# One-row load of `lower_bound`, turned on TensorE, and tile addresses moved to multiples of 512 bytes

## The chip, the cores and the metric

The kernel runs on one core of one Trainium2 chip. The metric is the device time of one execution in microseconds (us). Three runs of the kernel before took 201.95, 200.79 and 200.88 us; their median, 200.88 us, is the number to compare with.

## The reference

The computation has two parts. A gated recurrence runs along the sequence, for each of 4 batches and 256 channels, and its output goes through a soft mixture of experts with 32 slots (8 experts of 4). Cut to what matters:

```python
# x, f_logit: (4, 5056, 256); lower_bound: (256,); phi: (256, 32); w1: (8, 256, 1024); w2: (8, 1024, 256)
f = lower_bound + (1 - lower_bound) * sigmoid(f_logit)
i = 1 - f
for t in range(S):
    h = f[:, t] * h + i[:, t] * x[:, t]
    y[:, t] = h
logits = y.reshape(20224, 256) @ phi
d = softmax(logits, over the 20224 tokens);  c = softmax(logits, over the 32 slots)
slot_input = d.T @ y
slot_out = relu(slot_input @ w1) @ w2            # per expert
out = c @ slot_out                               # (20224, 256)
```

All inputs and the output are float32. `x` and `f_logit` are 20.7 MB each, the two weight arrays 8.4 MB each, the output 20.7 MB; `lower_bound` is 1 KB.

The kernel uses the identity 1 - f = (1 - lower_bound) * sigmoid(-f_logit). So `lower_bound` itself is needed only in two small constants per channel, `omlb` = 1 - lower_bound and `nomlb` = lower_bound - 1.

## The kernel before

**Tiling.** A unit of work is 512 tokens of one batch, 40 units in all, numbered n. The 256 channels are split as channel = 2p + o, so a partition p holds two neighbouring channels (`DC` = 2). Tokens arrive with tokens on the partitions, in 4 KB or 8 KB pieces per partition (`load`, L195 to L216). Per unit, ScalarE takes the sigmoid (`gate`, L226, tile `s_t`), GpSimd multiplies by x (`enter`, L237, tile `u_t`; the first unit is done by VectorE at L233), TensorE turns both to channels (L252, L258), ScalarE makes the decay `a` = 1 + nomlb * s (`decay`, L286 and L293), VectorE runs the scan (`scan`, L304), TensorE turns the result back to tokens (L317), a copy brings it to SBUF (L334), and TensorE makes the logits (L348) and adds up the slots (L398). Then come the experts (L590 to L686), and last the output: TensorE products (L704, L754), scaled by VectorE and ScalarE (L694, L759, L765), and stored by DMA.

**Order.** The order of all instructions on every engine is the order of the program text (`tc.manual_schedule()`). SP's queue issues the loads of `x` and `f_logit` and nearly all stores; ACT's queue issues the load of `lower_bound` (L75) and one store; GpSimd's queue issues `moe_phi` (L79) and the weights, which are converted from float32 to bfloat16 by the DMA on the way (L130, L140). The weights are issued among the late units, by the table `W_AT`. The tiles for `x` and `f_logit` are three deep, each holding two units.

**The start.** In program order: the load of `lb`, the load of `phi_f`, twelve loads for units 0 to 5 (`load(n, 1)`, 512 KB each, `f_logit` and `x` in turn), `lb_constants()`, then `gate(0)`, `enter(0)`, `s_to_channels(0)`, `decay(0)` for o = 0, and so on. `omlb` is used by `phi_constants` on GpSimd (L109) and by L598 and L599 late in the program. `nomlb` is the scale of every decay, first at L293 for unit 0. The PSUM pool `ptp` has a single buffer under the tag `tp`, used by `hp` in `to_tokens` (L317).

**Places in SBUF.** Pools are laid one after the other from the bottom of each partition's row: `consts`, `store`, `wts` (the weights), `ld` (the loaded `f_t` and `x_t`), and others above. Each tile's row is rounded up to 32 bytes. In the program before, `ident_f` begins at byte 16,512, `lb` at 17,792, `omlb` at 17,824, `nomlb` at 17,856, `phi_f` at 17,888, `etall` at 18,368, the first weight tile at 30,976 and the first `f_t` at 88,320. Once the weights are done, the output tiles `ob` and `oc` take the space from 30,976 on. From the first weight tile on, everything that a DMA reads or writes begins at 256 bytes past a multiple of 512.

Of the kernel before, what the change touches and what calls it, by code (L numbers as in the profile page):

```python
# [9 lines left out]
F32 = mybir.dt.float32  # L10
BF16 = mybir.dt.bfloat16
# [7 lines left out]
def kernel(  # L19
# [10 lines left out]
    nc = tc.nc  # L30
    B, S, D = x.shape
# [4 lines left out]
    P = 128  # L36
    DC = D // P
    FC = F // P
    R = 4
# [27 lines left out]
    consts = ctx.enter_context(tc.tile_pool(name="consts", bufs=1))  # L67
    ident_f = consts.tile([P, P], F32, name="ident_f")
# [2 lines left out]

    rep = consts.tile([P, B, NS], F32, name="rep")

    lb = consts.tile([P, DC], F32, name="lb")
    nc.scalar.dma_start(out=lb, in_=lower_bound.rearrange("(p o) -> p o", o=DC))  # L75
    omlb = consts.tile([P, DC], F32, name="omlb")
    nomlb = consts.tile([P, DC], F32, name="nomlb")
    phi_f = consts.tile([P, DC, NS], F32, name="phi_f")
    nc.gpsimd.dma_start(out=phi_f, in_=moe_phi.rearrange("(p o) s -> p o s", o=DC))  # L79
    phi = consts.tile([P, DC, NS], BF16, name="phi")  # L80
# [20 lines left out]
        nc.vector.memset(parity[ds(b * NS, NS), ds(b % 2, 1)], 1.0)  # L101

    def lb_constants():
        nc.vector.tensor_scalar(omlb, lb, -1.0, 1.0, ALU.mult, ALU.add)
        nc.vector.tensor_scalar(nomlb, lb, 1.0, -1.0, ALU.mult, ALU.add)

# [3 lines left out]


    store = ctx.enter_context(tc.tile_pool(name="store", bufs=1))
    etall = store.tile([P, S], BF16, name="etall")
    rrow = store.tile([P, n_grp * R, B], F32, name="rrow")
    left = store.tile([P, L, 2], BF16, name="left")
    nc.vector.memset(left, 0.0)
# [39 lines left out]
    with tc.tile_pool(name="sp2", bufs=3) as sp2, \  # L156
# [297 lines left out]
        for n in range(SINGLE):  # L454
            load(n, 1)
        lb_constants()
        gate(0, 1)
        enter(0)
# [368 lines left out]
```

## Time and profile before

| | |
|---|---|
| median of three runs | 200.88 us (200.79 to 201.95) |
| span of the profiled execution, first to last instruction | 198.1 us |
| lies outside the span, against the median | 2.8 us |
| busy: TensorE, VectorE, ScalarE, GpSimd | 153.3, 143.3, 138.7, 103.0 us |
| DMA packets | 14,448, 70.77 MB |
| HBM read, written | 58.23 MB, 20.71 MB |
| load of `lb`: issued, landed after | 0.72 us, 4.3 us |
| first `f_t` used (sigmoid of unit 0) | 4.85 us |
| first matmul | 6.05 us |

The profile is of one execution on the one core. Its span is what instructions cover; the time of that very execution beside the span isn't given, so that the 2.8 us between the span and the median of the other runs is taken to be what lies around a span. A "DMA share" in a row of windows is the busy share of the core's 16 DMA engines; as neighbouring packets overlap a little, a saturated stretch reads 1.02 to 1.07. The weights count in GB/s with what they write, half of what they read.

### The profile page before, as it was taken

The numbers are of one execution on the slowest core, as the hardware profiler recorded it, in microseconds if no ns is written. First come the engines' busy times: TensorE is split into PE (matmuls) and PEld (weight loads), VectorE is DVE, ScalarE is ACT, GpSimd is POOL, SyncE is SP. The second block draws the span as 40 slices with busy tenths as digits, with TensorE's granted clock in tenths as the row PEclk, the third lists the DMA queues.
The fourth block names the chain that finished last, engine by engine and source line by source line (L and its number), as shares of the span: only waits on it lengthen the run. The fifth ranks groups of instructions, "written<-read, shape, count | busy, mean of one in ns | idle before, by whom it ended". The sixth has DMA issues, their size and how long they took to land.

```text
span 198.1 us, 3497 instructions
## 1 busy us (share of the span) xinstructions
PE 153.3 (77%) x1330; PEld 110.4 (56%) x1330; DVE 143.3 (72%) x164; ACT 138.7 (70%) x195; POOL 103.0 (52%) x78
## 2 busy tenths in 40 slices
PE   0587599987999989898997978999989999950000
PEld 0366478776776768676695856568953543310000
DVE  1669869999699999999989999523268878840000
ACT  2688677899889999999897595622069889980000
POOL 2489578774998688884969969290030000000000
PEclk9999759997999999999999999999995555555555
DMA  5999999999999999999999999999639999999995
GB/s 177 418 420 419 427 429 429 427 427 357 378 424 424 408 337 420 432 411 307 407 420 392 241 215 214 213 212 211 110 110 419 430 421 427 450 443 424 424 424 218
DMA packets 14448, 70.77 MB, mean 357 GB/s; under 512 B 1744, under 2 KB 3024, under 8 KB 10464
## 3 DMA queue, kind: packets, MB, share of 16 engines
q1 hardware_dynamic: 11520, 62.00, 75.5%
q0 software_dynamic: 2624, 8.42, 21.3%
q8 instruction: 10, 0.16, 0.3%
q10 hardware_dynamic: 288, 0.13, 0.2%
q14 instruction: 6, 0.05, 0.1%
HBM read 58.23 MB, written 20.71 MB: 399 GB/s over the span
## 4 chain that ended last, share of the span: by engine, by line
PE 32%; DMA 30%; DVE 18%; POOL 6%; issue 3%; ACT 1%; ACTq 0%; SPq 0%; POOLq 0%
DMA x_t<-in_x_dram 15%; DVE h L304 13%; PE op L754 12%; DMA w_t<-in_moe_w_dram 8%; DMA w_sb<-in_moe_w_dram 7%; POOL u_t L237 5%; PE hp L317 4%; PE up L258 4%; PE sp L252 3%; DVE ht L334 3%; PE op L704 2%; PE slot_ps L174 2%; PE lg L348 1%; PE slot_ps L398 1%; DVE ob L694 1%
## 5 line engine op out<-in xcount | busy, mean ns | idle before, releaser
L237 POOL TENSOR_TENSOR u_t<-s_t,x_t 128x1024 bf16<-128x1024 bf16 (+1 forms) x39 | 82.5, 2128 | 23.3 <-ACT s_t L226 13.9
L304 DVE TENSOR_TENSOR_SCAN h<-a,h,up 128x512 bf16<-128x512 f32 (+1 forms) x72 | 86.9, 1252 | 4.7 <-PE up L258 2.5
L226 ACT ACTIVATE s_t<-f_t 128x2048 bf16<-128x2048 f32 (+2 forms) x23 | 38.3, 1668 | 5.8 <-DMA f_t<-in_f_logit_dram 4.5
L317 PE MATMUL hp<-ident_f,h 128*128 128x128 f32 (+1 forms) x160 | 29.5, 309 | 7.3 <-DVE ht L334 6.0
L317 PEld LDWEIGHTS hp<-ident_f,h 128*128 128x128 f32 (+1 forms) x160 | 23.1, 208 | 15.3 <-DVE ht L334 9.6
L252 PE MATMUL sp<-ident_f,s_t 128*128 128x128 f32 x144 | 22.6, 303 | 10.1 <-ACT s_t L226 7.8
L286 ACT ACTIVATE a<-sp,nomlb 128x1024 f32<-128x1024 bf16 x24 | 25.4, 1114 | 0.8 <-PE sp L252 0.6
L252 PEld LDWEIGHTS sp<-ident_f,s_t 128*128 128x128 f32 x144 | 18.6, 158 | 11.8 <-issue 6.0
L754 PE MATMUL op<-slot_bd,etall 64*128 64x512 bf16 x62 | 24.4, 600 | 0.1
L765 ACT ACTIVATE oc<-op,rrow 128x256 f32<-128x256 f32 x60 | 22.8, 490 | 1.4 <-PE op L754 0.9
L759 DVE TENSOR_TENSOR oc<-op,rrow 128x1024 f32<-128x1024 f32 x16 | 19.3, 1223 | 4.6 <-PE op L754 4.5
L293 ACT ACTIVATE a<-sp,nomlb 128x512 f32<-128x512 bf16 (+2 forms) x22 | 17.9, 859 | 4.8 <-PE sp L252 4.4
L258 PE MATMUL up<-ident_f,u_t 64*128 64x64 f32 x192 | 17.6, 229 | 2.0 <-POOL u_t L237 1.9
L174 PE MATMUL slot_ps<-rep,ident 128*128 128x256 bf16 x122 | 17.7, 281 | 0.0
L258 PEld LDWEIGHTS up<-ident_f,u_t 64*128 64x128 f32 x192 | 13.9, 138 | 5.9 <-POOL u_t L237 2.4
L754 PEld LDWEIGHTS <-etall 64*128 64x128 bf16 x62 | 9.0, 153 | 14.2 <-issue 11.6
L334 ACT COPY ht<-hp 128x512 f32<-128x512 f32 (+1 forms) x18 | 10.4, 580 | 8.0 <-PE hp L317 7.9
L334 DVE COPY ht<-hp 128x512 f32<-128x512 f32 (+1 forms) x22 | 14.7, 668 | 0.8 <-PE hp L317 0.8
L174 PEld LDWEIGHTS <-ident 128*128 128x128 bf16 x126 | 11.4, 102 | 3.4 <-issue 1.3
L304 DVE TENSOR_TENSOR_SCAN h<-a,up 128x512 bf16<-128x512 f32 x8 | 9.3, 1209 | 2.5 <-ACT a L293 1.8
L252 PE MATMUL up<-ident_f,u_t 128*128 128x128 f32 x48 | 9.8, 337 | 0.6 <-POOL u_t L237 0.6
L348 PE MATMUL lg<-h,phi 128*32 128x512 bf16 (+1 forms) x80 | 10.0, 411 | 0.0
(105 smaller groups left out, 147.8 us busy)
## 6 DMA issues: line engine op xcount, KB each, us to landing
f_t<-in_f_logit_dram SPq DMA_DIRECT2D x12, 1024.0 KB, 12.3
x_t<-in_x_dram SPq DMA_DIRECT2D x12, 1024.0 KB, 11.4
out_dram<-oc SPq DMA_DIRECT2D x6, 2048.0 KB, 13.1
w_sb<-in_moe_w_dram POOLq DMA_DIRECT2D x14, 512.0 KB, 10.3
f_t<-in_f_logit_dram SPq DMA_DIRECT2D x12, 512.0 KB, 8.6
x_t<-in_x_dram SPq DMA_DIRECT2D x12, 512.0 KB, 9.4
out_dram<-oc SPq DMA_DIRECT2D x4, 896.0 KB, 6.1
out_dram<-ob SPq DMA_DIRECT2D x1, 2048.0 KB, 8.9
```

Source lines behind the costliest of these rows:

```text
L174: nc.tensor.matmul(slot_bank[:, 1, ds(0, rhs.shape[1])], ident, rhs, start=first and i < 2, stop=False, skip_group_check=True)
L226: nc.scalar.activation(s_t, f_t, ACT.Sigmoid, scale=-1.0)
L237: nc.gpsimd.tensor_tensor(uts[n][:, :r], s_t[:, :r], x_t[:, :r], ALU.mult)
L252: nc.tensor.transpose(ps[:, :, r], t[:, r], ident_f)
L258: nc.tensor.transpose(v[:, :, r], t(r)[k].bitcast(F32), ident_f[k, k])
L286: nc.scalar.activation(a, sp[:, :, :, :, o], ACT.Identity, scale=nomlb[:, ds(o, 1)], bias=1.0)
L304: nc.vector.tensor_tensor_scan(h[:, :T, o], decays[n // 2, o][:, n % 2, :T], up[:, :T, o], hs[number(g - 1, b)][:, ds(used(g - 1) - 1, 1), ...
L317: nc.tensor.transpose(hp[:n_p, r], hw[:, :n_p, r], ident_f)
L334: copy(hts[g][:n_p, b].rearrange("p r d -> p (r d)").bitcast(F32), hps.pop(n)[:n_p].rearrange("p r c -> p (r c)"))
L754: nc.tensor.matmul(op[:, i_r].rearrange("p u d -> p (u d)"), ew[:, :, r + i_r], slot_bd[ds(j * 2 * NS, 2 * NS)].rearrange("s u d -> s (u d)"),
L759: nc.vector.tensor_tensor(ob[:, :, ds(r, k)].rearrange("p u r d -> p r u d"), op[:, ds(0, k)], scale[:, ds(r, k)].unsqueeze(3).broadcast_t ...
L765: nc.scalar.activation(ob[:, u, r + i_r], op[:, i_r, u], ACT.Copy, scale=scale[:, r + i_r, ds(u, 1)])
```

## The change

`lower_bound` is loaded as one row of 1 KB into partition 0 (`lb_row`) in place of 8 bytes into each of 128 partitions. `lb_constants` turns it to channels with two TensorE transposes, each of every second element of the row (1 x 128 to 128 x 1), into a PSUM tile under the tag `tp`. VectorE then reads `lb` from PSUM in its two instructions, whose results now share one tile `lbs`. `etall` is allocated with 160 more bfloat16 elements (320 bytes), which are not used.

```diff
-    lb = consts.tile([P, DC], F32, name="lb")
-    nc.scalar.dma_start(out=lb, in_=lower_bound.rearrange("(p o) -> p o", o=DC))
-    omlb = consts.tile([P, DC], F32, name="omlb")
-    nomlb = consts.tile([P, DC], F32, name="nomlb")
+    lb_row = consts.tile([1, D], F32, name="lb_row")
+    nc.scalar.dma_start(out=lb_row, in_=lower_bound.unsqueeze(0))
+    lbs = consts.tile([P, 2, DC], F32, name="lbs")
+    omlb, nomlb = lbs[:, 0], lbs[:, 1]
...
     def lb_constants():
+        row = lb_row.rearrange("u (p o) -> u p o", o=DC)
+        lb_ps = ptp.tile([P, R, P], F32, name="lb_ps", tag="tp")
+        lb = lb_ps[:, 0, ds(0, DC)]
+        for o in range(DC):
+            nc.tensor.transpose(lb_ps[:, 0, ds(o, 1)], row[:, :, o], ident_f[ds(0, 1), ds(0, 1)])
         nc.vector.tensor_scalar(omlb, lb, -1.0, 1.0, ALU.mult, ALU.add)
         nc.vector.tensor_scalar(nomlb, lb, 1.0, -1.0, ALU.mult, ALU.add)
...
-    etall = store.tile([P, S], BF16, name="etall")
+    PAD = 160
+    etall = store.tile([P, S + PAD], BF16, name="etall")[:, :S]
```

## The prediction, made before the changed kernel ran

> **What bounds the kernel now.** I read first the page's slices, for which resource never rests:
>
> ```profile
> span 198.1 us, 3497 instructions
> ...
> DMA  5999999999999999999999999999639999999995
> GB/s 177 418 420 419 427 429 429 427 427 357 378 424 424 408 337 420 432 411 307 407 420 392 241 215 214 213 212 211 110 110 419 430 421 427 450 443 424 424 424 218
> ...
> q1 hardware_dynamic: 11520, 62.00, 75.5%
> q0 software_dynamic: 2624, 8.42, 21.3%
> ```
>
> A slice is 198.1/40 = 4.95 us. The DMA engines are at 9 from the second slice to the 28th and again from the 31st; only the first, the 29th and 30th and the last are lower. The two queues alone fill 75.5 + 21.3 = 96.8% of 16 engines' span. The GB/s fall to 213 where weights are converted (they count with what they write, half of what they read), and to 307 to 378 where a weight mixes with loads. Then the windows view, by stage:
>
> ```profile
> 5.00:45.00 40.00, 32.21 (x223) 26.02 (x223) 33.49 (x37) 32.06 (x35) 29.87 (x20) 0.91 1.02 423
> 45.00:87.00 42.00, 38.47 (x377) 29.89 (x377) 39.69 (x37) 39.20 (x37) 33.47 (x18) 0.96 1.02 399
> 87.00:114.00 27.00, 24.29 (x235) 19.56 (x234) 26.39 (x27) 22.72 (x24) 22.21 (x18) 1.00 1.05 358
> ...
> 144.00:149.00 5.00, 4.31 (x30) 2.94 (x30) 3.50 (x6) 3.48 (x10) 1.84 (x2) 1.00 0.40 143
> 149.00:161.00 12.00, 12.00 (x38) 5.42 (x37) 10.20 (x10) 10.29 (x28) 0.00 (x0) 0.50 1.03 423
> 161.00:195.00 34.00, 15.13 (x39) 5.56 (x37) 12.06 (x10) 16.09 (x43) 0.00 (x0) 0.50 1.01 431
> ```
>
> Each row has the window, its length, the busy time of TensorE, its weight loads, VectorE, ScalarE and GpSimd, the clock, the DMA share, and GB/s. The share is over 1 up to 140 us (128 to 140 reads 1.07) and from 149 on. The chain of waits agrees at both ends: a load of `x` landing at 16.36, one at 35.14, then compute up to 113.3 (VectorE's scan, TensorE, GpSimd, with DMA full beside them), then 14.12 + 15.66 us of weights to 143.88, then the stores. So two things can move the end: the moment at which the saturated stretch begins, and the time of a packet within it. Work on an engine that neither delays a load nor the compute after 35 us costs nothing.
>
> The first five microseconds are not saturated:
>
> ```profile
> 1.70:2.10 0.40, 0.00 (x0) 0.00 (x0) 0.24 (x4) 0.40 (x1) 0.30 (x2) 1.00 0.47 164
> 2.10:2.50 0.40, 0.00 (x0) 0.00 (x0) 0.00 (x0) 0.34 (x1) 0.29 (x1) 1.00 0.26 92
> 2.50:3.00 0.50, 0.00 (x0) 0.00 (x0) 0.00 (x0) 0.00 (x0) 0.00 (x0) 1.00 0.86 271
> 3.00:3.50 0.50, 0.00 (x0) 0.00 (x0) 0.00 (x0) 0.00 (x0) 0.00 (x0) 1.00 0.83 213
> 3.50:4.00 0.50, 0.00 (x0) 0.00 (x0) 0.00 (x0) 0.00 (x0) 0.00 (x0) 1.00 0.81 279
> 4.00:4.50 0.50, 0.00 (x0) 0.00 (x0) 0.00 (x0) 0.00 (x0) 0.00 (x0) 1.00 1.05 402
> ```
>
> This is where the 128 packets of `lb`, 8 bytes each, pass: the trace's packet records have them from 2.12 to 4.47 us.
>
> **The removed load.** Eight small packets per engine at 9 ns each are 0.07 us: the least that their removal gives. The most is the whole deficit of the start: from 1.7 to 4.0 us the engines moved 210 GB/s where the next 2 us moved 414, so 2.3 x (1 - 210/414) = 1.1 us. Between them the records speak both ways. Before the first 8-byte packet, pairs of 4,096-byte packets run back to back (1.733 to 1.955, 1.952 to 2.111). From 2.1 to 2.5 each packet of `f_t` that starts after a pause starts 4 ns behind an 8-byte one (8 bytes at 2.369, 4,096 at 2.373), as if the engine had stood waiting for the small one. But from 4.0 to 4.25, 31 small packets pass with no loss of rate. I take the pauses alone, not the stretched packets (some 4,096-byte ones last 340 to 790 ns around 3 us, against 159): 0.74 x 0.4 = 0.30 us from 2.1 to 2.5, and 0.14, 0.17 and 0.19 of the next three half microseconds = 0.25 us. That is 0.55, say **0.5 us**; both ends stay for the range. It reaches the end undiminished: the loads behind are saturated, the compute chain hangs on the load landing at 35.14, and the stores hang on the last weights.
>
> **The added row.** It is 1 KB, at most 16 packets of 64 bytes or one of 1,024 (46 ns in the records), so at most one per engine or so: nothing. Its landing: the last 8-byte packet ended at 4.47 and `lb` was there at 5.02, 0.55 us later; the first one on each engine is done by about 2.9, so I estimate 3.4 us, and 5.0 at worst, as now.
>
> **Two transposes, and VectorE reading PSUM.** The nearest row is the transpose of L252 at the start, 4 in 1.08 us, 0.27 each, with much more data; two are 0.55 us at most. VectorE's two took 0.17 and 0.16. From 3.4 us: `omlb` and `nomlb` done by about 4.4. Who needs them: GpSimd's L109, which waits until 6.62 for `phi_f`; VectorE's own next work, L233 at 6.15; the first decay, L293 at 7.17, which waits for TensorE. TensorE itself does nothing before 6.05. All hidden. If the row lands at 5.0, the transposes end at 5.6 and `nomlb` at 6.0: still hidden. The `tp` buffer is next taken at 13.1 by `hp`. The added wait (TensorE on the row) holds back the four transposes of `s_t` of unit 0, and behind VectorE's wait stands L233; both have the slack just given.
>
> **SP's queue.** The waits view of SP has one row for the removed load:
>
> ```profile
> SPq L216 <- DMA lb<-in_lower_bound_dram: 0.8, 1, 0.8
> ```
>
> The eighth load of SP was issued at 5.01 instead of 4.21, when `lb` had landed. An earlier row lets it and the next go 0.5 to 0.8 us earlier. But six earlier loads of 512 KB are then under way, 3.1 MB or 7.4 us at 427 GB/s, and the load after those waits for `x_t` landing at 6.05 anyway: nothing gained. For the same reason a row that came a little late would cost nothing here.
>
> **The addresses.** `lb` (32 bytes with rounding) becomes 1,024: +992. The two constants share one row: -32. The padding: +320. Together +1,280, so the first weight tile goes from 30,976 to 32,256 = 63 x 512, and `f_t`, `x_t`, `ob`, `oc` with it, all tiles between being multiples of 512. (`lb_row` itself stays at 17,792 and `phi_f` goes to 18,848, neither a multiple of 512: the two small loads are not aligned.) So 174 us of saturated DMA get new addresses, and the trace has no packet of those at the new phase. Bounds: packets of 1,024 and 16,384 bytes last 46 and 611 ns, so a byte costs 565/15,360 ns, which is 27.2 bytes/ns, or 435 GB/s for 16 engines. Loads run at 427, weights at 2 x 213, stores at 431. If all that gap went, 109 us of loads gain 1.8% (2.0 us), 26 us of weights 2.1% (0.5), 47 us of stores 0.9% (0.4): **2.9 us**. On the other side, if each packet lost as much again as it loses now to that gap, 2.9 us more. I take **nothing**: the fixed part of a packet, 46 - 1,024/27.2 = 8 ns, is also what packets of 4 and 8 bytes last (9 ns), which cover no boundary that alignment could spare, and per-byte time leaves nothing over.
>
> The Trainium skill's page "DMA: Bandwidth & Descriptors", section "How a descriptor splits into AXI transactions", has a descriptor pay extra when it does not start on a multiple of 256 bytes. All large tiles are already at such multiples, so by this rule, too, the padding gives zero, and the sum would not change; no row here shows a packet off 256 against one on it. The same page's "Specifications" says that below 512 bytes an engine reads, modifies and writes; that speaks for dropping 8-byte pieces, but has no duration, and 16 pieces of 64 would still be below.
>
> **Sum.** Span 198.1 - 0.5 = 197.6; with the 2.8 us that the median of the runs has beyond the span, taken as unchanged, 200.4.
>
> **The rivals.** (1) *The start is slow by itself*, or the row is cut small again and stops the engines all the same: then only 0.07 us goes and it stays at 200.8. For it: the stretched packets around 3 us, and second-half engines that begin only at 2.5. Against: the pauses that end with an 8-byte packet. (2) *The new addresses speed every packet.* Half of the 2.9 with the 0.5 gives 200.9 - 2.0 = 198.9, all of both ends 200.9 - 4.0 = 196.9; call it 198.3. For it: so much of the span is packets. Against: the 8 ns that tiny packets show as well. It would also have to reach the end through 35 to 113 us, where compute is on the chain. (3) *The new addresses slow every packet*, the case on the other side: all of the mirrored 2.9 less 0.5 gives 203.3. It decides over 1% once 174 us of DMA get 2.5 us longer, 1.4%: loads at 421 GB/s in place of 427, a 4,096-byte packet at 161 ns in place of 159. Nothing in the trace speaks for it; nothing excludes it. (4) *The row lands late.* After 5.4 us it delays TensorE's first transposes one for one, but loads under way cover more than 7 us, so over 1% needs a landing past some 14 us, three times the 4.3 us that 128 packets take now.
>
> **How the numbers follow.** The forecast with 0.5 us from the start (0.1 to 1.1; its own range 199.8 to 200.8) has 0.48, rival 1 0.14, rival 2 0.26, rival 3 0.09, rival 4 0.03. Rival 2 is the case beyond 1% faster (under 198.9), rivals 3 and 4 the cases over 202.9; 1% is about what a measurement of this kernel can tell from no change. So faster 0.26, same 0.62, slower 0.12. The range 197.8 to 202.4 leaves out the far part of rival 2 (0.07) and rivals 3 and 4 (0.12).
>
> **What would show it.** In the changed profile: the packets of the row on the ACT queue, 16 or fewer, landing near 3.4 us; a DMA share between 2.1 and 4.0 us nearer 1, first sigmoid before 4.85 us, the last weights landing and the first store about 0.5 us earlier: the start. Packets of 4,096, 8,192 and 16,384 bytes at 159, 309 and 611 ns again and the stores at 431 GB/s: the addresses do nothing; other numbers there make rival 2 or 3 right and my step on the fixed part wrong. The first matmul of `s_t` at 6.0 or earlier: the transposes are hidden. A longer stretch between the same landmarks with unchanged packets would mean a compute effect that I have not seen.

## The result, and the profile after

The changed kernel takes 199.37 us (median of 22 runs, 199.0 to 200.22); the kernel before, over the same 22 runs beside it, 200.35 us (199.7 to 201.95). The ratio is 0.9939, with a 95% interval from 0.9924 to 0.9954: 0.9 to 1.5 us less. The forecast was 200.4 against a median before of 200.88, 0.5 us less, and its range 197.8 to 202.4.

The page of the changed kernel, the span, the slices and the ACT queue (q10), which issues the load of `lower_bound`:

```profile
span 197.6 us, 3501 instructions
...
DMA  5999999999999999999999999999639999999995
GB/s 207 418 418 422 427 426 426 428 428 347 392 426 421 387 354 425 425 407 306 414 416 369 257 219 213 213 214 212 109 142 394 430 421 425 444 448 431 425 425 216
...
q10 hardware_dynamic: 146, 0.13, 0.2%
```

The profiled span is 0.5 us shorter. In all 22 runs of the change 1.72 to 1.83 us lie between the span and the time, and in the runs of the kernel before that stand beside the experiments 1.72 to 1.85. So the 2.8 us taken for the kernel before is not what lies around a span: an execution with a span of 198.1 us takes about 199.9 us, and the profiled one before was half a microsecond faster than the median of its kernel, 200.35. The profiled one after, 199.36 us, lies at its median.

The slices look as before but for the first, 207 GB/s where it was 177: (207 - 177) x 4.95 us = 149 KB, or 0.35 us at 427 GB/s. On q10 there are 146 packets; 128 of the 1,024-byte ones belong to the store that was there before, and the row is one packet of 1,024 bytes, from 1.645 to 1.689 us.

The windows of the start, with the last two columns the DMA share and GB/s. Both count a packet in the window in which it starts, with its whole length, so packets that last long give a high share at a low rate:

```profile
1.70:2.10 0.40, 0.00 (x0) 0.00 (x0) 0.24 (x4) 0.40 (x1) 0.30 (x2) 1.00 0.64 82
2.10:2.50 0.40, 0.05 (x1) 0.05 (x1) 0.07 (x1) 0.40 (x1) 0.29 (x1) 1.00 0.66 92
2.50:3.00 0.50, 0.34 (x2) 0.26 (x2) 0.27 (x3) 0.06 (x1) 0.00 (x0) 1.00 0.72 262
3.00:3.50 0.50, 0.00 (x0) 0.00 (x0) 0.11 (x2) 0.00 (x0) 0.00 (x0) 1.00 1.00 410
3.50:4.00 0.50, 0.00 (x0) 0.00 (x0) 0.00 (x0) 0.00 (x0) 0.00 (x0) 1.00 1.07 434
...
161.00:195.00 34.00, 15.15 (x39) 5.55 (x37) 12.06 (x10) 16.11 (x43) 0.00 (x0) 0.50 1.02 435
```

Up to 3.0 us the start is no faster than before. The full rate is there from 3.0 us; before it took until 4.0. The last row is the long stretch of stores (431 before).

The timeline gives the transposes and those who wait behind them (start, duration, engine, line, operation; in brackets the idle time before and what ended it):

```profile
2.45 0.40 PE L108 MATMUL lb_ps<-ident_f,lb_row 1*128 1x1 f32 x2 [2.45 <-POOL ident_f masks.py:199]
...
2.88 0.16 DVE L109 TENSOR_SCALAR lbs<-lb_ps 128x2 f32<-128x2 f32 x1 [0.23 <-PE lb_ps L108]
2.96 0.15 DVE L110 TENSOR_SCALAR lbs<-lb_ps 128x2 f32<-128x2 f32 x1
...
4.37 1.06 ACT L232 ACTIVATE s_t<-f_t 128x1024 bf16<-128x1024 f32 x1 [1.81 <-DMA f_t<-in_f_logit_dram]
...
5.48 1.11 PE L258 MATMUL sp<-ident_f,s_t 128*128 128x128 f32 x4 [2.64 <-ACT s_t L232]
```

The transposes wait for the identity, not for the row, and the constants are done at 3.1 us, 2.4 us before TensorE has anything else to do. The first sigmoid starts at 4.37 in place of 4.85, the first matmul of unit 0 at 5.48 in place of 6.05. In the chain of waits (start and length of each piece, first of the kernel before, then of the changed one) the load of `x` that landed at 16.36 lands 0.47 us earlier (5.60 + 10.29 = 15.89), the one at 35.14 0.75 us earlier (34.39), and the last weights 0.72 us earlier (127.52 + 15.64 = 143.16; before 143.88):

```profile
6.06 10.30 DMA x_t<-in_x_dram
21.26 13.88 DMA x_t<-in_x_dram
128.21 15.66 DMA w_t<-in_moe_w_dram
```

```profile
5.60 10.29 DMA x_t<-in_x_dram
20.80 13.59 DMA x_t<-in_x_dram
112.64 14.59 DMA w_sb<-in_moe_w_dram
127.52 15.64 DMA w_t<-in_moe_w_dram
```

Of these 0.72 us the span keeps 0.48. In the changed profile the granted TensorE clock falls earlier (0.72 from 144 to 149 us, where it was 1.00), and from 149 to 161 us 407 GB/s move where it was 423; whether the clock is what cost the rest, no run shows:

```profile
144.00:149.00 5.00, 4.44 (x22) 2.63 (x23) 3.42 (x5) 3.14 (x8) 1.84 (x2) 0.72 0.55 205
149.00:161.00 12.00, 11.81 (x38) 5.29 (x36) 9.96 (x10) 10.28 (x27) 0.00 (x0) 0.50 0.99 407
```

### The profile page after: what moved, and what is told of

The parts are those of the page before. It is cut to its first block, busy times and chain, and to the rows that moved or that the text cites. A ratio compares the mean times of both kernels' runs of the same rounds, so it can differ in the third digit from the quotient of the medians.

```text
span 197.6 us, 3501 instructions
## 1 busy us (share of the span) xinstructions
PE 153.6 (78%) x1332; PEld 109.4 (55%) x1332; DVE 143.2 (72%) x164; ACT 138.4 (70%) x195; POOL 103.3 (52%) x78
## 4 chain that ended last, share of the span: by engine, by line
DMA 30%; PE 29%; DVE 16%; POOL 7%; ACT 5%; issue 3%; ACTq 0%; SPq 0%; POOLq 0%
DMA x_t<-in_x_dram 14%; DVE h L310 12%; PE op L760 12%; DMA w_t<-in_moe_w_dram 8%; DMA w_sb<-in_moe_w_dram 7%; POOL u_t L243 6%; PE hp L323 3%; PE op L710 3%; PE up L264 3%; DVE ht L340 3%; PE sp L258 3%; ACT oc L771 1%; PE slot_ps L180 1%; ACT a L292 1%; ACT s_t L232 1%
## 5 line engine op out<-in xcount | busy, mean ns | idle before, releaser
L292 ACT ACTIVATE a<-sp,lbs 128x1024 f32<-128x1024 bf16 x24 | 25.5, 1116 | 0.6 <-PE sp L258 0.6
L760 PE MATMUL op<-slot_bd,etall 64*128 64x512 bf16 x62 | 25.0, 620 | 0.2 <-ACT oc L771 0.2
L258 PEld LDWEIGHTS sp<-ident_f,s_t 128*128 128x128 f32 x144 | 17.8, 154 | 8.4 <-ACT s_t L232 5.4
L299 ACT ACTIVATE a<-sp,lbs 128x512 f32<-128x512 bf16 (+2 forms) x22 | 17.8, 859 | 4.6 <-PE sp L258 4.3
L180 PE MATMUL slot_ps<-rep,ident 128*128 128x256 bf16 x122 | 17.1, 274 | 0.0
```

The costliest lines, as they stand in the source:

```text
L180: nc.tensor.matmul(slot_bank[:, 1, ds(0, rhs.shape[1])], ident, rhs, start=first and i < 2, stop=False, skip_group_check=True)
L258: nc.tensor.transpose(ps[:, :, r], t[:, r], ident_f)
L292: nc.scalar.activation(a, sp[:, :, :, :, o], ACT.Identity, scale=nomlb[:, ds(o, 1)], bias=1.0)
L760: nc.tensor.matmul(op[:, i_r].rearrange("p u d -> p (u d)"), ew[:, :, r + i_r], slot_bd[ds(j * 2 * NS, 2 * NS)].rearrange("s u d -> s (u d)"),
```

## The experiments

Two theories stood after the result. S: all of the gain is the start, where small pieces of `lb` stood in the way of the first loads. A: the start gives only the 0.3 to 0.5 us that its rows show, and the new addresses give the rest. Each run below was timed in rounds beside the kernel before on the same chip (median before 200.35, 200.5 and 200.33 us in the three sets).

**One part at a time: the row with the old phase, the row without padding, the padding without the row.**

```diff
 # row_256                          # row_192                # pad_only, on the kernel before
-    PAD = 160                      -    PAD = 160            +    PAD = 128
+    PAD = 32                       +    PAD = 0              +    etall = store.tile([P, S + PAD], ...)[:, :S]
```

The first weight tile, and all large tiles above it, begin 256, 192 and 0 bytes past a multiple of 512.

> The row and its transposes, with 64 bytes of padding in place of 320: the large tiles are again at 256 past a multiple of 512, as before the change. Theory S (the start alone): the addresses do nothing, so this gains as much as the whole change, ratio to before near 0.994, and the span is 0.5 us or more shorter. Theory A (the start gives only the 0.3 to 0.5 us that the start rows show, the rest comes from the addresses): ratio 0.9975, some 0.5 us.

> The row and its transposes with no padding: the large tiles are at 192 past a multiple of 512, so off a multiple of 256 too. Theory S with packets indifferent to addresses: ratio near 0.994 again, packets of 4,096, 8,192 and 16,384 bytes at 159, 309 and 611 ns. If a start off 256 costs an extra piece per packet: packets longer by a few ns each, the loads below 427 GB/s, 1 to 3 us lost against the change, ratio 1.000 to 1.010.

> The kernel before with 256 bytes of padding: the large tiles at multiples of 512, the load of lb as 128 pieces. Theory S: same as before, ratio 0.999 to 1.001. Theory A: 0.5 to 0.7 us faster, ratio 0.9965 to 0.9975.

Measured: row_256 199.48 us, ratio 0.9962 (0.9941 to 0.9983). pad_only 200.36 us, ratio 0.9999 (0.9972 to 1.0026). So the row with the old phase has the gain (its median is 0.11 us above the change's), and multiples of 512 instead of 256 give nothing that these runs can see. The interval of row_256 alone would still allow theory A's 0.9975; pad_only, and the packets in the table below, speak against it. row_192 200.67 us, ratio 1.0031 (1.0003 to 1.0058): without the padding the row's gain is not only gone but turned into a loss.

**Off a multiple of 256 without the row.**

```diff
+    PAD = 32
-    etall = store.tile([P, S], BF16, name="etall")
+    etall = store.tile([P, S + PAD], BF16, name="etall")[:, :S]
```

> The kernel before with 64 bytes of padding: the large tiles at 320 past a multiple of 512, off 256. Packets indifferent to addresses: ratio 0.999 to 1.001. If a start off 256 costs an extra piece per packet: 1 to 3 us slower, ratio 1.005 to 1.015, with longer packets.

Measured: 202.1 us, ratio 1.0095 (1.0061 to 1.0129). The long stretches of loads and stores, in the windows of pad_64:

```profile
5.00:45.00 40.00, 31.85 (x222) 25.68 (x223) 33.02 (x37) 31.67 (x35) 29.79 (x20) 0.96 1.02 417
...
161.00:195.00 34.00, 16.44 (x42) 6.06 (x40) 13.24 (x11) 17.24 (x46) 0.00 (x0) 0.50 1.01 426
```

Before, these rows read 423 and 431 GB/s. The packet records say why (mean ns of a packet; the medians of 8,192 and 16,384 bytes are the 309 and 611 of the prediction wherever the start is on a multiple of 256; 4,096 bytes taken from 6 to 30 us; the last column is the converting load of weights, which writes 4,096 and reads 8,192 bytes):

```
            past 512   4,096   8,192   16,384   weights
before         256     159.1   310.9    611.5    323.7
row_256        256     159.0   310.8    611.5    323.7
pad_only         0     159.0   310.9    611.5    323.6
after            0     159.0   310.9    611.5    323.6
row_192        192     162.9   313.6    617.1    323.7
pad_64         320     162.4   313.6    617.3    323.6
```

Multiples of 256 and of 512 give the same to a tenth of a nanosecond. Off 256, loads into SBUF and stores out of it both lengthen by 3 to 6 ns a packet; the weights don't.

**The change again, the old pieces beside it, larger pieces beside it, and no load at all.**

```diff
 # row_and_8: the change, and the old load ahead of the row (whose line moves down to here)
+    nc.scalar.dma_start(out=slot_bd[:, 0, ds(0, 2 * DC)].bitcast(F32),
+                        in_=lower_bound.rearrange("(p o) -> p o", o=DC))
     nc.scalar.dma_start(out=lb_row, in_=lower_bound.unsqueeze(0))
 # row_and_512: in its place
+    nc.scalar.dma_start(out=slot_bd[:, 0].bitcast(F32), in_=moe_w1[0][ds(0, P), ds(0, P)])
 # no_lb, on the kernel before
-    nc.scalar.dma_start(out=lb, in_=lower_bound.rearrange("(p o) -> p o", o=DC))
+    nc.vector.memset(lb, 0.55)
```

> The whole change once more, beside the next three on one chip. Ratio near 0.994 as in its first runs (0.9924 to 0.9954).

> The whole change, and the old load of 128 pieces of 8 bytes issued ahead of the row on the same queue, into a tile that is overwritten late; its values are used by nothing. Theory S (the small packets stop the engines): the gain is gone, ratio 0.998 to 1.001, DMA share between 2.1 and 4.0 us back near 0.7 to 0.85, and steady rate from 4.0 us. If what helped was that lower_bound is there sooner: the gain stays within 0.2 us, ratio 0.994 to 0.996, since the row lands 1 us late at most.

> The whole change, and 128 pieces of 512 bytes of a weight array (used by nothing) issued ahead of the row. Their bytes are worth 64 KB at 427 GB/s, 0.15 us, with 8 ns per packet some 0.22 us. If it is the smallness of the pieces that stops the engines: 0.2 to 0.3 us slower than the change, ratio near 0.995 to 0.996. If any second queue with 128 pieces stops them: as slow as the old load or slower, ratio 0.999 to 1.002.

> The kernel before without the load of lower_bound: VectorE fills lb with 0.55 (the output is then that of another lower_bound); addresses as before. Theory S: as fast as the change or up to 0.2 us faster, ratio 0.992 to 0.995. Theory A: 0.3 to 0.5 us, ratio 0.9975.

Measured: after_again 199.39 us, ratio 0.9943 (0.9918 to 0.9968). row_and_8 200.21 us, 0.9997 (0.9966 to 1.0027): the gain is gone (by the medians 0.3 of 1.1 us is left, inside the interval). row_and_512 199.71 us, 0.9961 (0.9938 to 0.9983): 0.3 us behind the change by the medians, about what 64 KB and 128 packets last, though the intervals overlap. no_lb 199.39 us, 0.9953 (0.9933 to 0.9973), a hair above the expected 0.995: to have no load at all is no better than the row, so the row and its transposes cost nothing that can be measured. The start in the windows of row_and_8, then of no_lb:

```profile
2.10:2.50 0.40, 0.00 (x0) 0.00 (x0) 0.08 (x1) 0.40 (x1) 0.29 (x1) 1.00 0.99 92
2.50:3.00 0.50, 0.00 (x0) 0.00 (x0) 0.15 (x1) 0.50 (x1) 0.00 (x0) 1.00 0.79 148
3.00:3.50 0.50, 0.00 (x0) 0.00 (x0) 0.00 (x0) 0.01 (x1) 0.00 (x0) 1.00 0.73 287
3.50:4.00 0.50, 0.00 (x0) 0.00 (x0) 0.00 (x0) 0.00 (x0) 0.00 (x0) 1.00 1.08 388
```

```profile
2.10:2.50 0.40, 0.00 (x0) 0.00 (x0) 0.11 (x2) 0.00 (x0) 0.29 (x1) 1.00 0.17 72
2.50:3.00 0.50, 0.00 (x0) 0.00 (x0) 0.00 (x0) 0.00 (x0) 0.00 (x0) 1.00 0.88 352
3.00:3.50 0.50, 0.00 (x0) 0.00 (x0) 0.00 (x0) 0.00 (x0) 0.00 (x0) 1.00 0.99 410
```

With the pieces back (they pass from 2.76 to 4.52 us here), 148 and 287 GB/s between 2.5 and 3.5 us; without any load, 352 and 410. Between 2.1 and 2.5 the rate is low in both (92 and 72): that part of the slow start is not the pieces' doing. The DMA share was expected near 0.7 to 0.85; only two of the four windows have it. The whole stretch shows why, in the kernel before, after the change, and in row_and_8:

```profile
1.70:4.00 2.30, 0.00 (x0) 0.00 (x0) 0.24 (x4) 0.74 (x1) 0.59 (x2) 1.00 0.67 210
1.70:4.00 2.30, 0.40 (x2) 0.31 (x2) 0.69 (x7) 0.86 (x1) 0.60 (x2) 1.00 0.83 271
1.70:4.00 2.30, 0.00 (x0) 0.00 (x0) 0.46 (x5) 1.28 (x1) 0.59 (x2) 1.00 0.84 211
```

row_and_8 moves as little as the kernel before, but with the share of the changed one: the engines pause no more than after the change, and the loss lies in 4,096-byte packets that last longer.

One more rival can be weighed here. With the pieces, SP issues its seventh and eighth load late (5.06 and 5.43 us in row_and_8, 3.57 and 4.11 after the change), and that could be the loss. But row_and_512 issues them as late (4.97 and 5.34) and is 0.5 us faster than row_and_8 by the medians (the intervals overlap a little), so SP's delay is not what costs.

**The pieces where the engines are busy.**

```diff
         for n in range(n_unit):
+            if n == 10:
+                nc.scalar.dma_start(out=slot_bd[:, 0, ds(0, 2 * DC)].bitcast(F32),
+                                    in_=lower_bound.rearrange("(p o) -> p o", o=DC))
```

> The whole change, and the old load of 128 pieces of 8 bytes issued by ScalarE once more at unit 10 (some 25 to 35 us in, with the DMA engines full), into a tile that is overwritten late; used by nothing. If the small pieces stop the engines wherever they pass: the gain is gone as in the run with the small load at the start, ratio 0.998 to 1.001. If they cost only what they last, 8 x 9 ns per engine, because the start has nothing queued behind them to go on with: ratio 0.993 to 0.996, as the change.

Measured: 199.03 us (six runs), ratio 0.9929 (0.9912 to 0.9947), as fast as the change. The 128 pieces pass from 41.8 to 44.5 us, later than I had expected, and the window there keeps its rate (the change has 421 GB/s in the same window):

```profile
41.80:44.60 2.80, 2.34 (x26) 1.93 (x24) 2.30 (x4) 2.79 (x5) 2.77 (x3) 1.00 1.03 419
```

So the same 128 pieces cost 0.8 us by the medians and 1.1 by the ratios at the start (row_and_8 against after_again), and nothing that can be measured in the full stretch.

**Two tries at more of the start.**

```diff
 # x0_on_act
-    nc.sync.dma_start(out=t[:, ds(m % 2, 1)], in_=tokens(src, m, 1))
+    (nc.scalar if m == 0 and src is x else nc.sync).dma_start(...)
 # f0_halves
+    for c in range(0, P, P // 2 if m == 0 and src is f_logit else P):
+        half = ds(c, P // 2 if m == 0 and src is f_logit else P)
+        nc.sync.dma_start(out=t[half, ds(m % 2, 1)], in_=tokens(src, m, 1)[half])
```

> The whole change, with the first load of x issued on ACT's queue behind the row, in place of SP's. In the changed profile the second half of the engines gets its first packet of f_t at 2.48 us, 0.75 us after the first half. If a second queue feeds them sooner: up to 0.35 us faster than the change, ratio 0.992 to 0.993, and a DMA share nearer 1 from 1.7 to 2.5 us. If the pace at the start is set elsewhere: as the change, 0.994 to 0.995. A loss of 0.3 us or more would come from x and f_t sharing the engines, so that the first f_t lands later.

> The whole change, with the first load of f_logit split into two loads of 64 partitions each, both on SP. If each load's pieces go to all 16 engines, all of them begin at 1.7 us: up to 0.35 us faster than the change, ratio 0.992 to 0.993. If halves go to half the engines, or the additional issue (0.38 us of SP) delays the rest: the same or up to 0.3 us slower, 0.994 to 0.996.

Measured: x0_on_act 199.47 us, ratio 0.9961 (0.9946 to 0.9977); f0_halves 200.4 us, 1.0013 (0.999 to 1.0035). Neither gains; the second loses the whole of the change's gain, more than either of its expectations allowed. Its first packet starts at 2.40 us, where the change's starts at 1.73. Its timeline has the first sigmoid at 7.10 us in place of 4.37, of which 1.28 us is the load of ScalarE's function table, which there came only after the wait for the data:

```profile
5.81 1.28 ACT L234 ACT_TABLE_LOAD   x1 [5.81 <-DMA f_t<-in_f_logit_dram]
7.10 1.06 ACT L234 ACTIVATE s_t<-f_t 128x1024 bf16<-128x1024 f32 x1
```

How much of its loss is the table and how much the loads, which began late and ran slowly from 3 to 5.5 us (180 to 295 GB/s), was not separated. No version here beats the change by more than its interval.

## Why the prediction was right, and where its size was off

The packet records give one table: the time at which so many MB of loads on SP's queue had arrived, and the time of the last weight packet's completion, each less that of the kernel before (us; one execution of each):

```
              0.5 MB   8 MB   20 MB   40 MB   last weights   ratio
after          -0.33  -0.34   -0.35   -0.34      -0.72       0.9939
row_256        -0.44  -0.42   -0.44   -0.46      -0.84       0.9962
no_lb          -0.40  -0.38   -0.44   -0.37      -0.64       0.9953
late_8         -0.32  -0.35   -0.29   -0.30      -0.75       0.9929
after_again    -0.29  -0.27   -0.27   -0.30      -0.66       0.9943
x0_on_act      -0.31  -0.26   -0.28   -0.27      -0.68       0.9961
row_and_512    +0.14  +0.21   +0.20   +0.21      -0.25       0.9961
row_and_8      +0.07  +0.07   +0.03   +0.07      +0.17       0.9997
pad_only       +0.04  +0.09   +0.03   +0.06      -0.05       0.9999
row_192        -0.35  +0.03   +0.35   +0.83      +0.65       1.0031
pad_64         -0.03  +0.34   +0.70   +1.17      +1.34       1.0095
f0_halves      +0.56  +0.93   +0.90   +0.92      +0.28       1.0013
```

Here 0.5 MB is at 4.2 us and 40 MB at 105.7 us in the kernel before; x0_on_act counts its one load on ACT's queue too. The rows are read along the line: a lead that stays the same is a gain at the start, a lag that grows is a packet that lasts longer.

- *What bounds the kernel.* Right. A lead of a third of a microsecond, won by 4.2 us, is still there at 105.7 us (-0.33 and -0.34), and longer packets add up from end to end (pad_64: -0.03 to +1.17). Compute between 35 and 113 us absorbs neither.
- *The sum.* The span of 197.6 us that it gave is the profiled one, 197.6, and the 200.4 is 1.0 us above the measured 199.37, because the 2.8 us beyond the span are 1.8. That the span came out exactly is in part luck: the profiled execution before was half a microsecond faster than its median, and the change brought half a microsecond more than the sum had.
- *The removed load.* The mechanism was right: rival 1, that the start is slow by itself, fell with row_and_8 and no_lb, though up to 3.0 us the start is indeed slow by itself. The term is the one that was mis-sized: 0.5 us in the sum, and 1.0 us by the medians, 0.9 to 1.5 by the ratio; the upper end of 1.1 was nearer. Two steps behind it failed. The first step is "I take the pauses alone, not the stretched packets": row_and_8 has the pauses of the changed kernel and yet loses the gain, by packets that last longer, and after the change pauses and stretched packets are there too until 3.0 us. So the lead of the average engine, 0.34 us, is neither the 0.55 us of pauses nor the whole deficit of 1.1.
- *From the start to the end.* The second step is "It reaches the end undiminished": on the way to the last weights the lead did not stay as it was but grew. A load has landed when the last of its 16 completion marks is in the trace, and the landings lead by 0.47 us at 16 us and by 0.75 at 35, while the mean stays at 0.34. The load that landed at 35.14 us before has its last mark 1.9 us after the mean of its marks, after the change 1.5. It is 1.8 to 2.0 in the four programs that load the 8-byte pieces at the start (before, pad_only, pad_64, row_and_8), and 1.3 to 1.6 in all others. So what was won is above all with the last of the 16 engines, and the last weights, which start the stores, keep it (0.72). row_and_512 agrees: its loads are on the mean 0.2 us later and its last weights 0.25 us earlier, and it is faster than the kernel before. Why small pieces at the start hold back the last engine more, the traces don't show, as packets carry no engine there. Nor do they show where the median execution of the kernel before loses the half microsecond that its profiled one doesn't.
- *The row, its transposes, VectorE reading PSUM.* Right that they are hidden, and by more than I had said: the row's packet ended at 1.69 us, ahead of the identity (2.45), where I had estimated 3.4 for its landing, and no_lb is no faster.
- *SP's queue.* The wait of the eighth load for `lb` is gone (issued at 4.11), and the loads behind are on the mean no earlier than the third of a microsecond that was won before it.
- *The addresses.* Right: nothing, by pad_only and by the packet table. Rivals 2 and 3 are out: the packets did not change. The stretch of stores reads 435 GB/s where the sign asked for 431, but it reads 433 in row_256 at the old phase and 431 in pad_only at the new one, so it is no sign of the addresses. (The prediction speaks of 174 us of DMA where its three terms add up to 182; nothing hung on it.) The argument that tiny packets show the same fixed part held. What I passed over is what the padding does beside the row. The row, with its constants in one tile, moves all large tiles by 960 bytes, off a multiple of 256, and that alone would have cost 200.67 - 199.48 = 1.2 us (row_192 against row_256). So the padding has no worth of its own but keeps the row's worth; in the full change the two can't be added up from trials of each alone (0.9999 and 1.0031 against 0.9939).
- *The late row.* Out: it came at 1.7 us.

The rule of the Trainium skill's page "DMA: Bandwidth & Descriptors", "How a descriptor splits into AXI transactions", that a start off 256 bytes costs extra and one on it doesn't, agrees with the packet table for loads (162.4 and 162.9 ns against 159.0) and for stores (617.1 and 617.3 against 611.5); the packets of the weights, off 256 in SBUF in the same two runs, stayed at 323.6 and 323.7. In its beats (32 bytes, 1.2 ns at 27.2 bytes/ns) the bytes fetched in vain ahead of a store would be 192 for row_192 and 64 for pad_64, an estimate of 7 and 2 ns; measured were 5.6 and 5.8, so that the difference between the two, as the estimate has it, doesn't show. The 512 bytes in the same page's "Specifications" are a size of a piece, not an address, and no run here shows a gain from 512 as an address.

## What to carry to other kernels

In a kernel whose DMA engines never rest, look at the first microseconds as a stage of their own: 1 KB in 128 small pieces cost about 1 us there and nothing measurable once the engines were full, and one row, turned on an idle TensorE, was free. Whoever changes the size of an early tile moves every tile above it: check that the large ones still begin at a multiple of 256 bytes, since here 64 or 192 bytes off cost 0.7 to 1%, at least as much as the change brought. And what counts at the end of a saturated stretch is the engine that finishes last, so a mean rate can understate a gain by half (0.34 us on the mean, 0.72 at the last weights). And place the profiled execution among the timed ones before adding anything to its span: here it was half a microsecond off its median, as much as the term that was to be predicted.

## What the runs showed of the hardware that was not expected

- A single row of 1 KB into one partition went as one packet of 44 ns, which ended at 1.69 us, 0.97 us after its issue began at 0.72.
- 8-byte packets last 7 to 9 ns at the start and 9 at 42 us. At the start 128 of them cost about 1 us of the kernel's time (row_and_8 against after_again); at 42 us they left the rate at 419 GB/s, where the change has 421.
- Packets that begin off a multiple of 256 in SBUF are not all longer: in row_192 the median of the 16,384-byte stores is 615 ns and the slowest tenth 626 and more, against 611 for both on a multiple of 256. The weights, read as 8,192 bytes and written as 4,096, keep 323.7 ns.
- In the packet records about eight packets run at a time from 1.73 us on, and the others join at 2.48 us (2.51 before the change), as if half of the engines began later, with or without the small pieces. It isn't so in every execution: late_8, whose start is the changed kernel's, has twelve at a time from 2.1 us. Neither a second queue nor halves of the first load made the kernel faster.
